# Block masks turned two heads at a time and copied under the queries, filter work moved to other engines and earlier heads

## The chip, the cores and the metric

The kernel runs on one core of a Trainium2 chip. The metric is the time of one execution on the device in microseconds (us), lower is better, as a median of several runs. A core has five engines that follow their own instruction lists in order: TensorE (PE, matmuls), VectorE (DVE), ScalarE (ACT), GpSimd (POOL) and SyncE (SP), which here only issues DMAs. Engines wait for one another by semaphores. DMAs issued by SP share one hardware queue; those issued by POOL go through another.

## The reference

Two stages. The first is causal block-sparse attention: 4 batches of 8 heads, 768 positions, head size 64, so 32 heads in all. Keys are averaged in 12 blocks of 64. Each query scores the 12 block means, keeps the three best blocks that are not ahead of it and its own block, and attends to the keys in those blocks up to its own position:

```python
gate_scores = np.where(causal, einsum('bhsd,bhnd->bhsn', q, k_rep), -1e9)
top_idx = np.argsort(gate_scores, axis=-1)[..., -3:]   # and the own block
scores = np.where(mask & causal_by_position, scale * q @ k.T, -1e9)
attn_out = softmax(scores) @ v
```

The heads are put side by side (4 x 768 x 512) and go to the second stage, which convolves with a filter over the positions:

```python
x1, x2, x3 = split(x @ w_proj, 3)                   # 512 columns each
x2_conv = irfft(rfft(x2, axis=1) * rfft(filter_fft, axis=0))
out = (x1 * x2_conv * x3) @ w_out
```

## The kernel before, in words

**Attention, one head.** A head takes three slots, and a loop over all slots writes out the order of the work on every engine by hand. The 768 positions lie in six chunks of 128. In slot 0 of head n the loop issues loads for later heads, and for head n+3 `split_query` (DVE: a 16-bit query and its rest), `cast_key` and `low_query` (POOL: the 16-bit key, and the rest scaled). These land in `qk16`, of which there are three: per chunk 128 columns of query (64 high, 64 low) and 128 of key (64 of key, 12 that hold a one-hot of the key's block times 16384, zeros). In slot 1 `turn_query(n+3)` (L315) turns `qk16` by a DMA so that features lie on partitions: `qkT`, five buffers. In the same slot `gate(n+2)` (L331 to L343) multiplies the turned queries with the block sums of the keys (high and low halves give the precision that the choice of blocks needs), takes the best three on DVE and writes 0 or -1 per block into `qm16`, columns 64 to 75, beside a copy of the query that POOL makes (`mask_query`, L319). In slot 2 `turn_mask(n+2)` (L348) turns `qm16`, six blocks of 128x128, by another DMA.

`scores` (L375) multiplies 76 rows of the turned keys with 76 rows of the turned masked queries, so that a block that was not chosen gets -16384 before the exp. The scores are computed keys by queries, in three groups, one per slot, of 1024, 896 and 768 columns. ScalarE takes the exp (L378), POOL clears what lies ahead on the diagonal blocks (`diagonals`, L386), PE multiplies with the values in the next slot (`product`, L397), with a column of ones for the sums, ScalarE takes the inverse of the sums (L404, L405) and DVE scales (L415).

**Block sums.** `key_sums_mm`, `key_sums_copy`, `key_sums_turn`, `key_sums_split` prepare the sums for a group of heads: head 0, heads 1 to 3, 4 and 5, 6 and 7, then by fours.

**Second stage.** Its units are listed by slot in `first_plan` for batch 0, from slot 29 (slot 2 of head 9) to slot 49, and in `plan` for the others, 24 slots each. X2 projects x2, F1 and F2 are the forward and inverse transforms as matmuls with cosine and sine matrices, X13 projects x1 and x3, O is the output product. What they need is made by a table `setup` of (head, slot): `filter_rows` (L570 to L572) folds the filter's rows, `filter_spectrum` (L578 to L587) transforms them and writes the spectrum `Asb`, `Bsb`, `weights` (L596) loads and casts columns of the weights by POOL's DMAs, `inverse_part` (L234, L236) turns the cosine and sine matrices by DMA. The loop emits in a slot: scores, what earlier slots left for `later` (POOL's `PQ` and `yT` products among it), diagonals, the attention work above, `setup`, the units, and the product of the slot before.

**Queues.** SP issues in program order; an issue waits until its data is ready, and what follows on SP waits with it. PE, POOL, DVE and ScalarE are in order too.

Of the kernel before, what the change touches and what calls it, by code (L numbers as in the profile page):

```python
# [9 lines left out]
FP32 = mybir.dt.float32  # L10
# [7 lines left out]
def kernel(  # L18
# [76 lines left out]
    key_groups = [[0], [1, 2, 3], [4, 5], [6, 7]] + [list(range(m, m + KG))  # L95
# [20 lines left out]
    load_query(0)  # L116
    load_key(0)
    load_key(1)
    load_query(1)
    load_value(0)  # L120
    load_key(2)
    load_key(3)
# [28 lines left out]
    qk16s, qm16s, v16s = [], [], []  # L151
    for i in range(NB):
        qk16 = const.tile([P, SC, 2, P], fp, name=f"qk16_{i}")
        qk16s.append(qk16)
        qm16s.append(const.tile([P, SC, P], fp, name=f"qm16_{i}"))
        v16s.append(const.tile([P, SC, P], fp, name=f"v16_{i}"))

    def key_mask(i):
        nc.gpsimd.tensor_scalar(qk16s[i][:, :, 1, D:D + NBLK], in0=eblk, scalar1=MASK, scalar2=0.0,
                                op0=ALU.mult, op1=ALU.add)  # L160
# [7 lines left out]
    cbias = const.tile([P, SC, NBLK], FP32)  # L168

    ownm = const.tile([P, SC, NBLK], FP32)  # L170
# [3 lines left out]
    def small_constants():  # L174
        nc.gpsimd.memset(cbias, 0.0)
        nc.gpsimd.affine_select(
            out=cbias[0:64], in_=cbias[0:64], compare_op=ALU.is_ge,
            fill=-CBIG, base=0, pattern=[[2, SC], [-1, NBLK]], channel_multiplier=0)
        nc.gpsimd.affine_select(
            out=cbias[64:128], in_=cbias[64:128], compare_op=ALU.is_ge,  # L180
            fill=-CBIG, base=1, pattern=[[2, SC], [-1, NBLK]], channel_multiplier=0)
        nc.gpsimd.tensor_scalar(ownm, in0=eblk, scalar1=1.0, scalar2=-1.0,
                                op0=ALU.mult, op1=ALU.add)
# [31 lines left out]
    def sines(i):  # L215
# [3 lines left out]
        if i == 0:  # L219
# [76 lines left out]
    def cast_key(n):  # L296
        g, i = group_of[n]
        nc.gpsimd.tensor_copy(qk16s[n % NB][:, :, 1, 0:D], keys[g][:, i])
# [3 lines left out]
    def split_query(n):  # L302
        qk16 = qk16s[n % NB]
        q_nat = queries.pop(n)
        nc.vector.tensor_copy(qk16[:, :, 0, 0:D], q_nat)  # L305
        rems[n] = remp.tile([P, SC, D], FP32, name="rem", tag="rem")
        nc.vector.tensor_sub(rems[n], q_nat, qk16[:, :, 0, 0:D])  # L307

    def low_query(n):
        nc.gpsimd.tensor_scalar(qk16s[n % NB][:, :, 0, D:P], in0=rems.pop(n), scalar1=LO, scalar2=0.0,  # L310
                                op0=ALU.mult, op1=ALU.add)

    def turn_query(n):
        turned[n] = augp.tile([P, SC, 2, P], fp, name="qkT", tag="qkT")
        nc.sync.dma_start_transpose(turned[n].rearrange("p c t s -> p (c t) s"),  # L315
                                    qk16s[n % NB].rearrange("p c t s -> p (c t s)"))

    def mask_query(n):
        nc.gpsimd.tensor_copy(qm16s[n % NB][:, :, 0:D], qk16s[n % NB][:, :, 0, 0:D])  # L319
# [7 lines left out]
    def gate(n):  # L327

        gps = one_tile("gps", (P, GC * 2 * NBLK)).rearrange("p (c t n) -> p c t n", c=GC, t=2)
        for c in range(GC):  # L330
            nc.tensor.matmul(gps[:, c, :, :], lhsT=turned[n][:, c + 1, 0, :],  # L331
                             rhs=sums[group_of[n][0]][:, group_of[n][1], :, :],
                             start=True, stop=True)
        ga = small.tile([P, GC, NBLK], FP32, name="ga", tag="ga")
        nc.vector.tensor_add(ga, gps[:, :, 0, :], cbias[:, 1:SC, :])
        g = small.tile([P, GC, NBLK], FP32, name="g", tag="g")
        nc.vector.tensor_add(g, gps[:, :, 1, :], ga)
        m8 = small.tile([P, GC, 8], FP32, name="m8", tag="m8")
        for c in range(GC):
            nc.vector.max(m8[:, c, :], g[:, c, :])  # L340
        get = small.tile([P, GC, NBLK], FP32, name="get", tag="get")
        nc.vector.tensor_tensor(get, g, m8[:, :, 2:3].to_broadcast([P, GC, NBLK]), op=ALU.is_ge)
        nc.vector.scalar_tensor_tensor(out=qm16s[n % NB][:, 1:SC, D:D + NBLK], in0=get, scalar=-1.0,  # L343
                                       in1=ownm[:, 1:SC, :], op0=ALU.add, op1=ALU.max)

    def turn_mask(n):
        masks[n] = augp.tile([P, SC, P], fp, name="qmT", tag="qmT", bufs=4)
        nc.sync.dma_start_transpose(masks[n], qm16s[n % NB].rearrange("p c s -> p (c s)"))  # L348
# [21 lines left out]
    def scores(n, gi):  # L370
        pieces, lo, hi, _ = groups[gi]
        qT = masks[n].rearrange("p c s -> p (c s)")
        sps = big_tile("sps")
        for kc, qs, qe, col in pieces:
            nc.tensor.matmul(sps[:, col:col + qe - qs], lhsT=turned[n][0:76, kc, 1, :],  # L375
# [191 lines left out]
    def filter_rows(i):  # L567
# [3 lines left out]
        nc.vector.tensor_add(fil[:, 0, i, :], fa, rev)  # L571
        nc.vector.tensor_sub(fil[:, 1, i, :], fa, rev)  # L572

    def filter_spectrum(j):
# [9 lines left out]
        def put(dst, first, s0, second, s1, op):  # L584
            t = p2b.tile([P, Dm], FP32, name="turn", tag="t1")
            nc.vector.tensor_scalar(t, in0=second, scalar1=s1, scalar2=None, op0=ALU.mult)
# [16 lines left out]

    at(2, 1, turn_weights)
    at(4, 2, make_flip)
    for i in range(HC):
        at(i, 2, cosines, i)
        at(5 + i, 2, load_rows, i)
        at(7 + i, 0, filter_rows, i)
        at(10 + i, 2, inverse_part, i, False)  # L610
        at(10 + i, 2, inverse_part, i, True)
    for i, (n, slot) in enumerate([(9, 1), (10, 2), (11, 1)]):
        at(n, slot, filter_spectrum, i)
    for i in range(DC):
        dsl = slice(P * i, P * (i + 1))
        at(6 + (i + 1) // 2, 1, weights, wp, moe_w_proj, slice(Dm, 2 * Dm), slice(i, i + 1))
        n = [9, 10, 11, 12][i]
        at(n, 0, weights, wp, moe_w_proj, slice(P * i, P * (i + 1)), slice(0, DC))
        at(n, 1, weights, wp, moe_w_proj, slice(2 * Dm + P * i, 2 * Dm + P * (i + 1)), slice(0, DC))
        at(12 + i, 2, weights, wo, moe_w_out, slice(0, Dm), slice(i, i + 1))  # L620


    turn_angles()
    nc.vector.memset(lsc, 1.0)
    nc.vector.memset(lsc[64:128, :], 1.0 / LO)
    for i in range(NB):
        nc.vector.memset(qk16s[i][:, :, 1, D + NBLK:P], 0.0)
# [12 lines left out]
    load_query(2)  # L640
    key_sums_mm(0, range(SC))
    key_sums_copy(0)
    key_sums_turn(0)
    sines(1)
    small_constants()
    key_sums_split(0)
    phase_round(2)
    phase_turns(2)
    key_mask(1)
    split_query(1)  # L650
    cast_key(1)
    low_query(1)
    turn_query(1)
    load_key(4)
    load_key(5)
    key_sums_mm(1, range(SC))
    sines(2)
    nc.scalar.activation(tw, twf, AF.Sin, bias=0.0, scale=math.pi / S)

    nc.scalar.preload_act_table_set("natural_log_exp_and_others")  # L660
    for i in range(NB):
        nc.gpsimd.memset(qm16s[i][:, :, D:P], 0.0)
    mask_query(0)
    gate(0)
    turn_mask(0)
    nc.gpsimd.memset(v16s[0][:, :, D:P], 1.0)
    cast_value(0)
    key_mask(2)
    load_query(3)
    load_value(1)  # L670
    key_sums_copy(1)
    key_sums_turn(1)
# [4 lines left out]
    key_sums_split(1)  # L677
    gate(1)
    mask_query(1)
    turn_mask(1)  # L680
    for i in range(1, NB):
        nc.gpsimd.memset(v16s[i][:, :, D:P], 1.0)
    mask_query(2)
# [4 lines left out]
    for slot in range(max(units) + 1):  # L688
# [10 lines left out]
        if n < NH:  # L699
            diagonals(n, s)  # L700
            if s == 0:
# [3 lines left out]
                if n + 4 < NH:  # L705
                    load_query(n + 4)
# [4 lines left out]
                if n + 3 < NH:  # L711
                    split_query(n + 3)
                    cast_key(n + 3)
                    low_query(n + 3)
                if n + 2 in group_at and n:
                    key_sums_split(group_at[n + 2])
            elif s == 1:
                if n + 3 < NH:
                    turn_query(n + 3)
                if n + 2 < NH:  # L720
                    gate(n + 2)
            else:
                if n + 2 < NH:
                    turn_mask(n + 2)
                if n + 3 < NH:
                    mask_query(n + 3)
# [55 lines left out]
```

## Time and profile before

| | us |
|---|---|
| median of three runs | 330.61 |
| lowest, highest | 329.84, 330.74 |
| the profiled execution, in all | 328.21 |
| its span | 326.5 |
| mean granted clock of PE | 0.932 of full |

| engine | busy us | share of the span |
|---|---|---|
| PE | 256.4 | 79% |
| DVE | 227.2 | 70% |
| ACT | 196.3 | 60% |
| POOL | 191.5 | 59% |

The profile is one execution. Its page gives busy time by engine, the span in 40 equal slices, the chain of work that ended last, and the costliest groups of instructions. L with a number is a line of the kernel. Other views list the waits, the instructions in order of time, or the busy time in a stretch. "DMA share" is the mean busy share of the 16 DMA engines; as it sums the time of packets that overlap, it can pass 1. Times in the text such as "scores of head 10 at 93.6" are starts from the span's beginning, read from the timeline.

### The profile page before, as it was taken

The page shows a single profiled execution, that of the slowest core. Times are in us where ns is not written, and L with a number is a line of the kernel's source. Part 1 is how long each engine was busy: PE and PEld are TensorE (multiplying, and loading weights), DVE is VectorE, ACT ScalarE, POOL GpSimd, SP SyncE. Part 2 cuts the span into 40 slices and gives each one's busy share as a digit, 9 for nine tenths or more (in the row PEclk, how much of TensorE's full clock was granted, in tenths as well). Part 3 has the DMA queues.
Part 4 walks back from the last instruction along what each step waited for, and adds up shares of the span by engine and source line. Part 5 has one row for each costly group of instructions (what it writes and reads, how often), then busy time and mean ns, then how long its engine had stood idle before and what let it go on. Part 6 is the DMA issues. An engine that isn't in the chain of part 4 may idle for free.

```text
span 326.5 us, 5163 instructions
## 1 busy us (share of the span) xinstructions
PE 256.4 (79%) x1531; PEld 132.9 (41%) x1531; DVE 227.2 (70%) x637; ACT 196.3 (60%) x314; POOL 191.5 (59%) x360
## 2 busy tenths in 40 slices
PE   3567687665989585995499787997997889899785
PEld 2233333232344242552144444553444446445442
DVE  6557867535799994689247898788678976537650
ACT  2247787663445453586367956688867669943234
POOL 6646747644244778576534587678645876703770
PEclk9959989775899998999589999999999999999999
DMA  9999999999999959797677977687996471021005
GB/s 168 182 206 181 217 218 199 201 219 218 167 147 158 145 103 177 154 132 151 135 163 168 214 151 160 113 140 155 220 200 156 99 125 24 2 103 58 34 1 193
DMA packets 163260, 48.65 MB, mean 149 GB/s; under 512 B 158368, under 2 KB 159392, under 8 KB 163232
## 3 DMA queue, kind: packets, MB, share of 16 engines
q1 hardware_dynamic: 157856, 46.22, 72.6%
q0 software_dynamic: 5376, 2.10, 6.0%
q8 instruction: 12, 0.20, 0.2%
q14 instruction: 16, 0.13, 0.1%
HBM read 24.64 MB, written 6.29 MB: 95 GB/s over the span
## 4 chain that ended last, share of the span: by engine, by line
PE 44%; DVE 18%; DMA 14%; ACT 8%; issue 7%; POOL 6%; SPq 1%; DVEq 0%; ACTq 0%; POOLq 0%
DMA qkT<-qk 10%; PE oT L397 7%; PE krp L266 6%; PE sps L375 5%; PE op L515 5%; PE x13b L482 4%; PE x2a L443 3%; PE x2b L443 3%; PE x13a L482 2%; DVE xT L415 2%; ACT den L404 2%; ACT ex L378 2%; ACT den L405 2%; DVE gx L487 2%; DVE t L464 2%
## 5 line engine op out<-in xcount | busy, mean ns | idle before, releaser
L378 ACT ACTIVATE ex<-sps 128x1024 f16<-128x1024 f32 (+2 forms) x96 | 87.4, 917 | 30.5 <-PE sps L375 28.5
L386 POOL TENSOR_SCALAR_AFFINE_SELECT ex<-ex 128x128 f16<-128x128 f16 (+1 forms) x128 | 46.7, 377 | 82.7 <-ACT ex L378 81.8
L397 PE MATMUL oT<-ex,v 128*128 128x384 f16 (+2 forms) x288 | 57.7, 308 | 3.7 <-POOL ex L386 1.9
L375 PE MATMUL sps<-qmT,qkT 76*128 76x384 f16 (+2 forms) x288 | 57.0, 311 | 0.9 <-DMA qmT<-qm 0.9
L415 DVE TENSOR_TENSOR xT<-oT,den 64x384 f16<-64x384 f32 x64 | 35.2, 550 | 27.8 <-ACT den L405 26.3
L404 ACT ACTIVATE den<-oT 64x384 f32<-64x384 f32 x64 | 31.1, 485 | 37.8 <-PE oT L397 35.8
L397 PEld LDWEIGHTS <-v 128*128 128x128 f16 x288 | 27.4, 102 | 39.0 <-issue 20.8
L482 PEld LDWEIGHTS <-wp 128*128 128x128 f16 x256 | 24.3, 97 | 28.9 <-issue 14.0
L405 ACT ACTIVATE den<-den 64x384 f32<-64x384 f32 x64 | 33.3, 520 | 2.0
L266 PE MATMUL krp<-k_nat,eblk 128*12 128x256 f32 (+3 forms) x120 | 29.2, 382 | 5.3 <-issue 2.0
L375 PEld LDWEIGHTS <-qkT 76*128 76x128 f16 x288 | 27.2, 104 | 13.0 <-issue 3.4
L515 PE MATMUL op<-wo,yT 128*128 128x512 f16 x96 | 25.6, 392 | 8.1 <-DMA wo<-in_moe_w_out_dram 6.1
L482 PE MATMUL x13b<-xT,wp 128*128 128x384 f16 x116 | 23.6, 326 | 6.1 <-ACT x1sb L486 4.0
L471 POOL TENSOR_TENSOR PQ<-t,t 128x512 f16<-128x512 f32 x12 | 15.2, 1271 | 21.0 <-DVE t L464 20.6
L482 PE MATMUL x13a<-xT,wp 128*128 128x384 f16 x116 | 23.6, 326 | 4.1 <-DVE t L467 3.9
L305 DVE CAST qk<-q_nat 128x384 f16<-128x384 f32 x32 | 18.8, 587 | 10.9 <-issue 4.5
L518 ACT COPY osb<-op 128x512 f32<-128x512 f32 x24 | 14.0, 585 | 18.7 <-PE op L515 17.6
L307 DVE TENSOR_TENSOR rem<-q_nat,qk 128x384 f32<-128x384 f32 x32 | 22.8, 714 | 2.4
L310 POOL TENSOR_SCALAR qk<-rem 128x384 f16<-128x384 f32 x32 | 16.3, 510 | 11.1 <-DVE rem L307 8.9
L331 PE MATMUL gps<-kr,qkT 128*128 128x24 f16 x160 | 9.1, 176 | 16.8 <-DMA qkT<-qk 15.8
L507 POOL TENSOR_TENSOR yT<-gx,yy 128x384 f16<-128x384 f32 x16 | 16.0, 999 | 10.0 <-DVE yy L503 9.7
L486 ACT CAST x1sb<-x13a 128x384 f16<-128x384 f32 x29 | 13.8, 476 | 12.4 <-PE x13a L482 12.4
(122 smaller groups left out, 432.3 us busy)
## 6 DMA issues: line engine op xcount, KB each, us to landing
q_nat<-in_q_dram SPq DMA_DIRECT2D x32, 192.0 KB, 3.5
k_nat<-in_k_dram SPq DMA_DIRECT2D x32, 192.0 KB, 3.2
v_nat<-in_v_dram SPq DMA_DIRECT2D x32, 192.0 KB, 3.7
out_dram<-osb SPq DMA_DIRECT2D x24, 256.0 KB, 2.1
wp<-in_moe_w_proj_dram POOLq DMA_DIRECT2D x12, 128.0 KB, 5.1
fa<-in_moe_filter_fft_dram SPq DMA_DIRECT2D x3, 256.0 KB, 3.1
fb<-in_moe_filter_fft_dram SPq DMA_DIRECT2D x3, 256.0 KB, 4.1
qkT<-qk SPq DMA_TRANSPOSE x32, 4.4
```

What stands on the lines that cost most here:

```text
L266: nc.tensor.matmul(sums[g][0:NBLK, 0:w * D], lhsT=eblk[:, c, :], rhs=keys[g][:, 0:w, c, :], start=(c == 0), stop=(c == SC - 1))
L307: nc.vector.tensor_sub(rems[n], q_nat, qk16[:, :, 0, 0:D])
L375: nc.tensor.matmul(sps[:, col:col + qe - qs], lhsT=turned[n][0:76, kc, 1, :], rhs=qT[0:76, qs:qe], start=True, stop=True, skip_group_check ...
L378: nc.scalar.activation(ex[:, lo:hi], sps[:, lo:hi], AF.Exp, bias=0.0, scale=scale)
L386: nc.gpsimd.affine_select(out=sub, in_=sub, compare_op=ALU.is_ge, fill=0.0, base=0, pattern=[[0, cnt], [1, P]], channel_multiplier=-1)
L397: nc.tensor.matmul(oT[:, qs - HALF * half:qe - HALF * half], lhsT=vals[n][:, kc, :], rhs=exps[n, src][:, col:col + qe - qs], start=first, ...
L404: nc.scalar.activation(den[64:128, :], oT[64:128, :], AF.Ln, bias=0.0, scale=1.0)
L405: nc.scalar.activation(den[64:128, :], den[64:128, :], AF.Exp, bias=0.0, scale=-1.0)
L415: nc.vector.tensor_tensor(out=dst, in0=oT[0:64, :], in1=den[64:128, :], op=ALU.mult)
L443: nc.tensor.matmul(pp, lhsT=xT[:, dc, base + P * i:base + P * (i + 1)], rhs=wp[:, dc, Dm:2 * Dm], start=(dc == 0), stop=(dc == DC - 1))
L482: nc.tensor.matmul(dst, lhsT=wp[:, dc2, base:base + P], rhs=xT[:, dc2, hs:hs + HALF], start=(dc2 == 0), stop=(dc2 == DC - 1))
L515: nc.tensor.matmul(op, lhsT=yT[:, cc, P * scn:P * (scn + 1)], rhs=wo[:, cc, :], start=(cc == 0), stop=(cc == DC - 1))
```

## The change

**Masks.** `gate` takes a list of one or two heads and writes their masks side by side into `gm16` (24 columns, two buffers); one DMA (`turn_mask`) turns both. The turned query's low half is needed by the gate alone, so its rows 64 to 75 are then overwritten with the mask rows by a small DMA within the core's memory (`place_mask`, 12 partitions x 768), and `scores` reads the turned query itself. `qm16` and POOL's `mask_query` are gone. Heads 0 and 1 have their masks turned on PE and copied by ScalarE (`turn_first_mask`). From then on, for even n, heads n+2 and n+3 share `gate` (slot 1 of head n) and `turn_mask` (slot 2); their two `place_mask` stand in slot 1 of head n+1. For heads 2 and 3 gate and turn stand in slot 2 of head 0.

**Order.** Queries and keys are prepared four heads ahead and not three; the queries' layout is by kind and then chunk. Loads at the start are query and key of heads 0, 1, 2 first, and the key groups become [0], [1], [2, 3], and so on.

**Filter.** ScalarE copies the flipped rows out of PSUM, POOL adds and subtracts; in the spectrum ScalarE does the product that DVE did. These run in heads 4 to 8 in place of 7 to 11, the cosine and sine turns in heads 8 to 10 (before 10 to 12), the weights' columns in heads 8 to 11 (before 9 to 12), the output weights in heads 11 to 14 (before 12 to 15).

```diff
-    key_groups = [[0], [1, 2, 3], [4, 5], [6, 7]] + [list(range(m, m + KG))
+    key_groups = [[0], [1], [2, 3], [4, 5], [6, 7]] + [list(range(m, m + KG))
...
-    load_query(0)
-    load_key(0)
-    load_key(1)
-    load_query(1)
-    load_value(0)
-    load_key(2)
-    load_key(3)
+    for n in range(3):
+        load_query(n)
+        load_key(n)
...
     def turn_query(n):
-        turned[n] = augp.tile([P, SC, 2, P], fp, name="qkT", tag="qkT")
-        nc.sync.dma_start_transpose(turned[n].rearrange("p c t s -> p (c t) s"),
-                                    qk16s[n % NB].rearrange("p c t s -> p (c t s)"))
-
-    def mask_query(n):
-        nc.gpsimd.tensor_copy(qm16s[n % NB][:, :, 0:D], qk16s[n % NB][:, :, 0, 0:D])
+        turned[n] = augp.tile([P, 2, SC, P], fp, name="qkT", tag="qkT")
+        nc.sync.dma_start_transpose(turned[n].rearrange("p t c s -> p (t c) s"),
+                                    qk16s[n % NB].rearrange("p t c s -> p (t c s)"))
...
-    def turn_mask(n):
-        masks[n] = augp.tile([P, SC, P], fp, name="qmT", tag="qmT", bufs=4)
-        nc.sync.dma_start_transpose(masks[n], qm16s[n % NB].rearrange("p c s -> p (c s)"))
+    def turn_mask(ns):
+        gmT = augp.tile([P, SC, P], fp, name="gmT", tag="gmT", bufs=2)
+        nc.sync.dma_start_transpose(gmT, gm16s[(ns[0] + len(ns)) // 2 % 2].rearrange("p c s -> p (c s)"))
+        for h, n in enumerate(ns):
+            masks[n] = gmT[h * NBLK:(h + 1) * NBLK]
+
+    def turn_first_mask(n):
+
+        gmp = ps_one.tile([P, S], fp, name="gmp", tag="one", padded_shape=[P, 2 * 512])
+        for c in range(SC):
+            nc.tensor.transpose(gmp[0:NBLK, P * c:P * (c + 1)],
+                                gm16s[(n + 1) // 2 % 2][:, c, 0:NBLK], id_f16)
+        nc.scalar.copy(turned[n][D:D + NBLK, 0],
+                       gmp[0:NBLK, :].rearrange("n (c s) -> n c s", c=SC))
+
+    def place_mask(n):
+
+
+        nc.sync.dma_start(turned[n][D:D + NBLK, 0], masks.pop(n))
...
-        qT = masks[n].rearrange("p c s -> p (c s)")
+        qT = turned[n][:, 0].rearrange("p c s -> p (c s)")
...
-        nc.vector.tensor_add(fil[:, 0, i, :], fa, rev)
-        nc.vector.tensor_sub(fil[:, 1, i, :], fa, rev)
+        nc.scalar.copy(fb, rev)
+        nc.gpsimd.tensor_add(fil[:, 0, i, :], fa, fb)
+        nc.gpsimd.tensor_sub(fil[:, 1, i, :], fa, fb)
...
-            nc.vector.tensor_scalar(t, in0=second, scalar1=s1, scalar2=None, op0=ALU.mult)
+            nc.scalar.mul(t, second, s1)
...
+    at(0, 2, gate, [2, 3])
+    at(0, 2, turn_mask, [2, 3])
...
-        at(5 + i, 2, load_rows, i)
-        at(7 + i, 0, filter_rows, i)
-        at(10 + i, 2, inverse_part, i, False)
-        at(10 + i, 2, inverse_part, i, True)
-    for i, (n, slot) in enumerate([(9, 1), (10, 2), (11, 1)]):
-        at(n, slot, filter_spectrum, i)
+        at(2 + i, 2, load_rows, i)
+        at(4 + i, 1, filter_rows, i)
+        at(6 + i, 2, filter_spectrum, i)
+        at(8 + i, 2, inverse_part, i, False)
+        at(8 + i, 2, inverse_part, i, True)
...
-        n = [9, 10, 11, 12][i]
+        n = 8 + i
...
-        at(12 + i, 2, weights, wo, moe_w_out, slice(0, Dm), slice(i, i + 1))
+        at(11 + i, 2, weights, wo, moe_w_out, slice(0, Dm), slice(i, i + 1))
...
-                if n + 4 < NH:
-                    load_query(n + 4)
+                if n + 5 < NH:
+                    load_query(n + 5)
...
-                if n + 3 < NH:
-                    split_query(n + 3)
-                    cast_key(n + 3)
-                    low_query(n + 3)
+                if n + 4 < NH:
+                    split_query(n + 4)
+                    cast_key(n + 4)
+                    low_query(n + 4)
...
-                if n + 3 < NH:
-                    turn_query(n + 3)
-                if n + 2 < NH:
-                    gate(n + 2)
+                if n + 4 < NH:
+                    turn_query(n + 4)
+                if n % 2 == 0 and 0 < n < NH - 2:
+                    gate([n + 2, n + 3])
+                elif n % 2 == 1 and n + 1 < NH:
+                    place_mask(n + 1)
+                    place_mask(n + 2)
             else:
-                if n + 2 < NH:
-                    turn_mask(n + 2)
-                if n + 3 < NH:
-                    mask_query(n + 3)
+                if n % 2 == 0 and 0 < n < NH - 2:
+                    turn_mask([n + 2, n + 3])
```

## The prediction

> **What bounds the kernel now.** I read the page's slices, then the chain of waits in order of time, then the span cut head by head (busy time by stretch), last the timelines of SP, POOL and PE around one head. The columns of the first view are 40 slices of 8.2 us.
>
> ```profile
> PEclk9959989775899998999589999999999999999999
> DMA  9999999999999959797677977687996471021005
> ```
>
> For the first 14 slices (to about 115 us) the DMA engines are full, while the units of the second part start only in slot 2 of head 9. The chain says what the queue holds up:
>
> ```profile
> 22.44 5.06 DMA qkT<-qk
> 28.06 5.51 DMA qkT<-qk
> 34.59 4.41 DMA qkT<-qk
> ...
> 52.75 5.95 DMA qkT<-qk
> 59.88 6.26 DMA qkT<-qk
> ...
> 68.59 6.57 DMA qkT<-qk
> ...
> 124.49 4.20 DMA IC<-FC
> ...
> 156.66 3.00 DMA wo<-in_moe_w_out_dram
> ```
>
> To 75 us the end is set by the turns of queries and keys (T(n), L315): `gate(n+2)`, in slot 1 of head n, waits for T(n+2). After that single DMAs stand in the chain: the IC turn, and the last `wo` weight.
>
> Below, one stretch per head, from its first scores matmul to the next head's: heads 11, 13, 15, 16, then 19, 21, 23, 24, which have the same units one batch later (19 as 11, and so on). Columns: length, then busy us of PE, PEld, DVE, ACT, POOL, the clock, DMA share, GB/s.
>
> ```profile
> 103.00:115.20 12.20, 8.54 (x52) 4.27 (x50) 11.49 (x27) 5.24 (x8) 7.64 (x12) 1.00 0.97 156
> ...
> 124.60:137.90 13.30, 10.73 (x60) 5.18 (x58) 6.88 (x21) 6.20 (x10) 8.39 (x15) 0.87 0.97 158
> ...
> 144.90:152.40 7.50, 5.03 (x40) 3.01 (x38) 7.20 (x16) 4.31 (x8) 5.48 (x10) 1.00 0.76 157
> 152.40:167.40 15.00, 8.91 (x41) 4.12 (x39) 6.01 (x18) 7.59 (x12) 7.35 (x14) 0.66 0.77 157
> ```
> ```profile
> 183.30:191.80 8.50, 6.54 (x46) 3.69 (x44) 7.48 (x21) 6.22 (x10) 5.99 (x10) 1.00 0.76 165
> ...
> 201.90:211.10 9.20, 9.20 (x60) 4.65 (x58) 7.20 (x21) 6.19 (x10) 7.55 (x14) 1.00 0.67 130
> 211.10:218.10 7.00, 6.45 (x50) 3.84 (x48) 5.97 (x19) 5.85 (x10) 4.44 (x10) 1.00 0.85 121
> 218.10:223.80 5.70, 5.01 (x39) 3.00 (x37) 5.41 (x15) 4.28 (x9) 5.26 (x10) 1.00 0.81 165
> 223.80:231.60 7.80, 6.42 (x42) 3.16 (x39) 5.88 (x17) 6.89 (x12) 5.60 (x10) 1.00 0.92 198
> ```
>
> Heads 10 to 16 take 73.9 us. Their twins: head 10's three units cost as head 18 (6.8) and a little more, 7.5; head 12 as head 20 (10.1) less one output unit (0.9), 9.2; then 8.5, 9.2, 7.0, 5.7, 7.8: together 55. So 19 us of heads 10 to 16 are filter work, the wait for IC (head 13) and the 6.1 us that PE waits for `wo` (head 16).
>
> **The change part by part.** My sum is against the profiled execution: 326.5 us span, 328.21 in all, which is 2.4 below the median of the runs.
>
> *Heads 0 and 1.* The first mask loses its DMA turn (issued 14.62, landed 17.69) and takes six PE transposes (nearest row L282, 0.21 each) and a ScalarE copy of 768 columns (nearest row an exp of 768, 0.81). But both first masks now stand ahead of the first scores on PE: the gate of head 1, its 1.9 us on DVE, then six more transposes. POOL's identity and larger constants (about 1 us) lie beside DVE's work. I put the first scores at 18 us, as now (17.7); bounds 16.5 and 20.
>
> *Heads 2 to 9.* Loads come as 256-byte packets (192 KB: 768), and T(n) is 12 blocks of 128 rows, 1,536 packets; the old mask turn is 768. That makes 4,608 per head, 147,456 of the page's 157,856 on queue 1. Up to T(3), 1,248 packets per engine, landed 27.5; up to T(8), 2,736, landed 58.7: 21 ns each, 6.0 us per head. Now a pair needs one mask turn instead of two: 528 per engine for two heads, 11.1 us instead of 12.1. That is the gain. The loss is what must be through the queue before a head starts. Today the scores of head n need T(n+1). Now `place_mask` for heads n+1 and n+2 is issued in slot 1 of odd head n, on SP behind T(n+4); the scores of n+1 wait for it, and PE with them. Head 2 thus needs everything up to T(5): 1,536 per engine, 1.5 + 32.1 = 33.6, and about 1.3 for the copy: 35, today 30.1.
>
> From there it is a loop and no longer a stream: T(n+4) waits for POOL's `low_query(n+4)`, which stands behind the diagonal masks of head n's slot 0, so behind its scores and exp. In head 23:
>
> ```profile
> 222.05 0.50 POOL L298 CAST qk<-k_nat 128x384 f16<-128x384 f32 x1
> 222.64 0.51 POOL L310 TENSOR_SCALAR qk<-rem 128x384 f16<-128x384 f32 x1
> ```
> ```profile
> 223.18 1.44 SPq L315 DMA_TRANSPOSE qkT<-qk  x1
> ```
>
> Scores 218.1, `low_query` done 223.15, T issued 223.18, landed 226.85; the scores of head 24 began at 223.81, and with the copy behind T would have to wait past 227. So an odd head lasts at least (scores to `low_query`) + (T's issue to the copy's landing). The first is 4.0 to 5.7 in the odd heads read from the timelines (4.0, 4.5, 5.3, 4.8 in heads 1 to 7; 5.7 in 15; 5.0 in 23). The second is in no row. T itself lands 3.6 after issue at best, 4.4 in the median, 9.0 at worst; the nearest row for the copy is an output store, 2.0 at best after its own issue, and the copy's issue is 1.5 behind T's. So at least 3.6; I take 4.2 where the queue is free, being T's row plus one more item, and 5 in the early heads; upper bound 9.5.
>
> The Trainium skill, page "DMA: Bandwidth & Descriptors", section "Anatomy of one DMA — SWDGE (gpsimd) path", gives every DMA a fixed cost of about 2 us whatever its bytes, fitted on the software path, and so speaks against small copies; the 18 KB copy would by that be an estimated 2.04 us, 3.5 behind T's issue, each of some eleven odd heads 0.7 shorter than I reckon, and the sum below −12.7 in place of −5.0. No run here shows a copy of this size.
>
> Early odd heads then last 9.5 (4.5 + 5), even ones about 5 (head 2: 30.1 to 35.1 today): 14.5 per pair instead of the stream's 12.1. Heads 4 and 6 add a `rev` product (L570, 1.8 us of PE), 6 and 8 a filter spectrum (six matmuls, 1.6), and heads 8 and 9 the weights (1.4 us of queue each): pairs of 14.5, 16, 16, 16.5 from head 2. Scores of head 10 at 98, today 93.6: +4.4. With the queue empty at each copy the stream could be at 94; with 1 us more in each pair, 102.
>
> *Filter, by engine.* POOL's add and subtract (nearest row L471, 1.27 each, three pairs: 7.6) sit in slot 1 of heads 4 to 6 and may push `low_query` of the next head by 1 or so; ScalarE's copies (0.58 each) and seven products lie under the same waits. SP's third pair of row loads waits for POOL's first pair. All costed at nothing because the copy's wait covers them; without that cover, some 5 us.
>
> *Heads 10 to 16.* The filter is gone from here (7 `turn` and 7 `put` on DVE, 10 us, on the path in heads 9, 11); IC and IS turns come two heads sooner, `wo` one head sooner, ahead of the `yT` products that hold POOL at 153 to 156. So 73.9 becomes 55, but with the odd head's least time: head 11, 4.0 + 4.2, +1 for the weights in the queue; head 13, 5.2 + 4.2 against 9.2; head 15, 5.75 less `mask_query` (0.6, off POOL) + 4.2 = 9.3 against 5.7. Together 60: −13.9.
>
> *Heads 17 to 31.* `mask_query` leaves POOL (19.1 us in all) and the paired gate saves DVE 0.2 per head, neither on the path, which is PE's. The copy's wait: head 23, 5.0 − 0.6 + 4.2 = 8.6 against 5.7, +2.9; head 25, T landed 6.4 after issue among output stores, +1.6; heads 17, 19, 21, 27 between 7.9 and 8.6, against 8.5 to 9.2, nothing; 29 has no T ahead. +4.5; bounds 0 and 10. The tail from 285 is untouched.
>
> Sum: +4.4 − 13.9 + 4.5 = −5.0: 323.2, and by the median of the runs 325.6.
>
> **Rivals.**
> *The copy binds harder (slower).* If T's issue to the copy's landing takes 1.5 more than I reckon, 5.7 and early 6.5 (T lands 4.4 to 6.6 in the chain above), four early pairs lose 6 us and heads 11 to 27 about 10: 325.6 + 16 = 341.6. It decides from about 0.5 us later than I reckon, since some eleven heads carry it. For it: the early turns. Against: after 160 us T lands 3.7 in most heads.
> *The copy is hidden (much faster).* If POOL reaches `low_query` 2 us sooner, head 10 starts at 94 and the later waits vanish: −19, so 312. Against: POOL waits for ScalarE's exp (81.8 us of its idle time), not for itself.
> *The filter disturbs the early heads.* POOL holds `low_query` behind the filter's waits for PE, ScalarE and the row loads: 5 to 6 us more by head 10, about 331, no change.
>
> **How the numbers follow.** Forecast 0.5, harder copy 0.22, hidden copy 0.15, disturbed 0.13. About 0.3% (1 us) is what a measurement can tell from no change. Faster: 0.47 + 0.15 + 0.04; same 0.03 + 0.05 + 0.02; slower the rest. Range: below, half of the hidden case is left out, 315; above, most of the harder one is kept, 335. The likeliest case alone runs from 320 to 330.
>
> **What would show it.** Right: scores of head 2 near 35, of head 10 near 98, of head 17 near 158; PE idle before the scores of even heads until the copy lands; no wait for `wo` or IC. Wrong: the even heads' scores do not wait, or T's issue to the copy's landing is over 5 in heads 17 to 27; heads 10 to 16 over 64 us.

## The result, and the profile after

The changed kernel takes 347.8 us (median; 345.0 to 349.3), the kernel before, run beside it, 330.2. The ratio is 1.054 with a 95% interval of 1.045 to 1.064: 5% slower, where 325.6 was forecast and 335 was the upper end. The profiled execution has a span of 345.7 us and a mean granted clock of 0.904 (before 326.5 and 0.932). Times here and below are medians of all executions, while the ratios leave out the few executions in a slower state, at most two of a run.

First the page of the changed kernel: clock and DMA share in 40 slices, now of 8.6 us, and the shares of the chain that ended last.

```profile
PEclk9996876787769699899969999999699999999999
DMA  8796979998569889768778686667866511021004
...
PE 42%; POOL 14%; ACT 13%; DVE 11%; DMA 10%; issue 7%; SPq 4%; DVEq 0%; ACTq 0%; POOLq 0%
```

The row of DMA shares no longer begins with fourteen nines: the stream that bounded the first 115 us is gone. The clock row has the new trouble, a 6, 7 or 8 in most slices from 26 to 112 us. The next view is the list of waits: waiting engine and line, what it waited for, then the total in us, how often, and the longest.

```profile
PE sps L393 <- DMA qkT<-gmT: 33.8, 10, 6.0
...
DVE qk L302 <- DMA q_nat<-in_q_dram: 10.2, 2, 7.7
```

PE waits 33.8 us for the small copy of the mask rows under the turned queries (`qkT<-gmT`). The chain of waits has that copy ahead of head after head; its columns are start, length and what was waited for:

```profile
39.04 2.18 DMA qkT<-gmT
...
55.46 2.10 DMA qkT<-gmT
...
71.86 2.26 DMA qkT<-gmT
...
91.28 4.37 DMA qkT<-gmT
...
112.48 3.29 DMA qkT<-gmT
...
133.76 5.77 DMA qkT<-gmT
...
172.68 2.39 DMA qkT<-gmT
...
239.78 2.36 DMA qkT<-gmT
...
272.75 2.39 DMA qkT<-gmT
```

Before each of them lies what SP did. In SP's timeline of head 11 ("SPq" is the queue's own issue) the copies leave when the issue of the next queries' turn T(15) is done, although their mask had been turned a head earlier:

```profile
131.03 2.63 SPq L312 DMA_TRANSPOSE qkT<-qk  x1
133.76 2.06 SPq L366 DMA_DIRECT2D qkT<-gmT  x2
```

The scores of head 12 start at 139.58, 8.6 us after T's issue. The forecast beside the measured, in starts of first scores and in lengths (us):

| | before | forecast | after | missed by |
|---|---|---|---|---|
| scores of head 2 start | 30.1 | 35 | 41.3 | 6.3 |
| heads 2 and 3 | 13.0 | 14.5 | 16.4 | 1.9 |
| heads 4 and 5 | 11.3 | 16 | 16.6 | 0.6 |
| heads 6 and 7 | 13.5 | 16 | 21.5 | 5.5 |
| heads 8 and 9 | 25.6 | 16.5 | 20.1 | 3.6 |
| heads 10 to 16 | 73.8 | 60 | 67.7 | 7.7 |
| head 17 to the end | 159.0 | 163.5 | 162.2 | −1.3 |
| span | 326.5 | 321.5 | 345.7 | 24.2 |

So three quarters of the miss lies in front of head 10. A stage read from one execution is good to 1 us at best: a later run, the same program up to head 8, has that head's scores at 94.9, the changed kernel at 95.7. In the early heads of the kernel before it is worse: the filter's half alone (below), the same program up to slot 2 of head 2, reaches head 2 at 32.7 and not 30.1.

### The profile page after: what moved, and what is told of

Same layout as the page of the kernel before. It is cut to its first block, busy times and chain, and to the rows that moved or that the text cites. A ratio compares the mean times of both kernels' runs of the same rounds, so it can differ in the third digit from the quotient of the medians.

```text
span 345.7 us, 5124 instructions
## 1 busy us (share of the span) xinstructions
PE 268.8 (78%) x1555; PEld 138.3 (40%) x1555; DVE 206.4 (60%) x568; ACT 204.4 (59%) x326; POOL 186.1 (54%) x336
## 4 chain that ended last, share of the span: by engine, by line
PE 42%; POOL 14%; ACT 13%; DVE 11%; DMA 10%; issue 7%; SPq 4%; DVEq 0%; ACTq 0%; POOLq 0%
DMA qkT<-gmT 8%; PE sps L393 7%; PE oT L415 6%; PE op L533 5%; ACT ex L396 4%; PE krp L263 4%; SPq L312 3%; ACT den L422 3%; PE x2a L461 3%; PE x2b L461 2%; POOL ex L404 2%; PE x13b L500 2%; PE x13a L500 2%; ACT den L423 2%; POOL PQ L489 1%
## 5 line engine op out<-in xcount | busy, mean ns | idle before, releaser
L396 ACT ACTIVATE ex<-sps 128x1024 f16<-128x1024 f32 (+2 forms) x96 | 88.0, 917 | 59.4 <-PE sps L393 57.4
L393 PE MATMUL sps<-qkT 76*128 76x384 f16 (+2 forms) x288 | 62.2, 332 | 33.8 <-DMA qkT<-gmT 33.8
L415 PE MATMUL oT<-ex,v 128*128 128x384 f16 (+2 forms) x288 | 59.7, 314 | 11.6 <-POOL ex L404 6.5
L263 PE MATMUL krp<-k_nat,eblk 128*12 128x256 f32 (+2 forms) x132 | 28.3, 356 | 1.9 <-POOL dft_ka L205 1.6
L533 PE MATMUL op<-wo,yT 128*128 128x512 f16 x96 | 27.2, 416 | 2.0 <-POOL yT L525 1.8
L500 PE MATMUL x13a<-xT,wp 128*128 128x384 f16 x116 | 24.3, 332 | 0.0
L302 DVE CAST qk<-q_nat 128x384 f16<-128x384 f32 x32 | 17.9, 559 | 10.4 <-DMA q_nat<-in_q_dram 10.2
L505 DVE TENSOR_TENSOR gx<-x1sb,x13b 128x384 f32<-128x384 f16 x29 | 16.0, 551 | 12.5 <-PE x13b L500 8.3
L304 DVE TENSOR_TENSOR rem<-q_nat,qk 128x384 f32<-128x384 f32 x32 | 21.2, 664 | 2.5
L317 POOL CAST v<-v_nat 128x384 f16<-128x384 f32 x32 | 19.0, 593 | 0.0
```

Of the source, the lines that this page charges most:

```text
L263: nc.tensor.matmul(sums[g][0:NBLK, 0:w * D], lhsT=eblk[:, c, :], rhs=keys[g][:, 0:w, c, :], start=(c == 0), stop=(c == SC - 1))
L304: nc.vector.tensor_sub(rems[n], q_nat, qk16[:, 0, :, 0:D])
L317: nc.gpsimd.tensor_copy(vals[n][:, :, 0:D], values.pop(n))
L396: nc.scalar.activation(ex[:, lo:hi], sps[:, lo:hi], AF.Exp, bias=0.0, scale=scale)
L415: nc.tensor.matmul(oT[:, qs - HALF * half:qe - HALF * half], lhsT=vals[n][:, kc, :], rhs=exps[n, src][:, col:col + qe - qs], start=first, ...
L500: nc.tensor.matmul(dst, lhsT=wp[:, dc2, base:base + P], rhs=xT[:, dc2, hs:hs + HALF], start=(dc2 == 0), stop=(dc2 == DC - 1))
```

## The experiments

The expectations call the theory that the copies' place behind T sets the time C, and the theory that the moved filter work does it F, with numbers for their variants. Two more came out of the trace: the first heads wait for query 4's load, and PE runs at half clock after each wait. Ratios below are to the kernel before, run beside each, with 95% intervals. Its median lay between 328.9 and 331.4 us in these rounds, so one or two microseconds between runs of different rounds mean little.

### The copies ahead of T

In slot 1 of odd heads the two copies are issued before the turn of queries n+4:

```diff
             elif s == 1:
+                if n % 2 == 1 and n + 1 < NH:
+                    place_mask(n + 1)
+                    place_mask(n + 2)
                 if n + 4 < NH:
                     turn_query(n + 4)
                 if n % 2 == 0 and 0 < n < NH - 2:
                     gate([n + 2, n + 3])
-                elif n % 2 == 1 and n + 1 < NH:
-                    place_mask(n + 1)
-                    place_mask(n + 2)
```

> The changed kernel, with one order turned round: in slot 1 of odd heads the two mask copies are issued on SP ahead of the query turn T(n+4) instead of behind it. Theory C (the copy behind T is the cost): PE's waits for the copy before even heads, 33.8 us in ten waits, shrink to under 8 us in all; 347.8 falls by 20 to 33, to 315 to 328. Rival F (the filter on POOL and ScalarE in heads 4 to 8 holds the early heads): the waits turn into waits for other work, the time stays over 338. Rival S (the start alone is late): head 2 still starts near 39 to 41 and less than 10 us are gained.

Measured: 323.3 us, ratio 0.974 [0.968, 0.980]. Two lines changed places, and 24.5 us are gone: the change is now 2.6% faster than the kernel before. SP's timeline of this run, in slot 1 of head 11:

```profile
120.31 1.59 SPq L366 DMA_DIRECT2D qkT<-gmT  x2
122.00 2.24 SPq L312 DMA_TRANSPOSE qkT<-qk  x1
```

In the kernel as changed the copies sat out T's own issue (2.6 us in this head) and, in heads such as 7, 15 and 23, T's wait for POOL's `low_query` before it. Here they leave 1.7 us before T does, in head 13 3.1. Head 15 shortens from 9.4 to 6.6 us, head 23 from 8.8 to 5.7 (before: 7.5 and 5.7). The waits of this run:

```profile
PE sps L393 <- DMA qkT<-gmT: 14.7, 5, 4.0
```

They were to fall below 8 and fell to 14.7. What is left are the waits of heads 2, 4, 6, 10 and 12, and in the chain of this run their copies take longer than any quiet one above:

```profile
36.35 3.57 DMA qkT<-gmT
...
51.05 3.70 DMA qkT<-gmT
...
65.70 4.41 DMA qkT<-gmT
...
100.91 5.12 DMA qkT<-gmT
...
120.31 5.11 DMA qkT<-gmT
```

Loads, turns and weights are in the queues at that time; which of these holds the copies was not tried. By stage the swap is worth 1.3 by the start of head 2, then 8.4 in heads 2 to 9, 10.3 in heads 10 to 16, and 6.3 in the rest. That last stage is now 155.9 against 159.0 before, about 1 us less in each of heads 19, 24 and 27. The filter's half alone leaves it at 159.0, so the 3.1 us are what the masks' half is worth there once nothing waits; `mask_query`, the halved gates and the longer lead were not tried apart.

### Each half alone

The masks' half alone has the change, but the filter's engines and slots of the kernel before:

```diff
-        nc.scalar.copy(fb, rev)
-        nc.gpsimd.tensor_add(fil[:, 0, i, :], fa, fb)
-        nc.gpsimd.tensor_sub(fil[:, 1, i, :], fa, fb)
+        nc.vector.tensor_add(fil[:, 0, i, :], fa, rev)
+        nc.vector.tensor_sub(fil[:, 1, i, :], fa, rev)
...
-            nc.scalar.mul(t, second, s1)
+            nc.vector.tensor_scalar(t, in0=second, scalar1=s1, scalar2=None, op0=ALU.mult)
...
-        at(2 + i, 2, load_rows, i)
-        at(4 + i, 1, filter_rows, i)
-        at(6 + i, 2, filter_spectrum, i)
-        at(8 + i, 2, inverse_part, i, False)
-        at(8 + i, 2, inverse_part, i, True)
+        at(5 + i, 2, load_rows, i)
+        at(7 + i, 0, filter_rows, i)
+        at(10 + i, 2, inverse_part, i, False)
+        at(10 + i, 2, inverse_part, i, True)
+    for i, (n, slot) in enumerate([(9, 1), (10, 2), (11, 1)]):
+        at(n, slot, filter_spectrum, i)
```

with the slots of the weights and of `make_flip` back as well. The filter's half alone is the same edit the other way round, on the kernel before.

> The masks' half of the change alone: masks of two heads in one turn and the copies stay, while the filter's work, its engines, the weights and the cosine and sine turns stand where they were before the change. Theory C: the copy's waits stay, the relief of heads 10 to 16 is gone, so 350 to 360, slower than the whole change. Rival F: without the filter in heads 4 to 8 scores of head 10 come 9 us or more sooner than 115.8 and the time is under 346.

> The other half alone: the kernel before, with its masks and query turns, and only the filter folded by ScalarE and POOL in heads 4 to 8, the cosine and sine turns two heads sooner and the weights one head sooner. Theory C: this half is a gain by itself, as the sum had it: the waits for wo and IC go, head 10 starts by 96, heads 10 to 16 last 56 to 60 instead of 73.9; 314 to 322. Rival F: POOL's part holds the query turns of heads 5 to 9, head 10 starts after 100, and the time is 325 or more.

Masks alone: 342.9 us, 1.034 [1.027, 1.040]. Filter alone: 321.6 us, 0.970 [0.964, 0.977]. The first is 7 us better than C gave it and inside the time that F gave it, though head 10 comes only 6.9 us sooner (109.0), not 9: the moved filter costs something where the masks' half has made a loop. The two halves multiplied make 1.003, the whole 1.054: the 5%, some 17 us, belong to neither half but to their meeting. By the intervals that is roughly 12 to 21 us. In the four profiled spans it is 8.9: 6.6 in heads 2 to 9 and 6.0 in heads 10 to 16, less 3.2 ahead of head 2, where single executions differ as said above, and 0.6 at the end. Drawing the filter and the weights forward costs 0.8 us in heads 2 to 9 of the kernel before (64.3 for 63.5), which go by the DMA stream, and 7.4 with the new masks (74.5 for 67.1). Read from the start of head 10 it is 3.4 (97.0 for 93.6) and 6.9 (115.8 for 109.0); the direction is the same, the size is good to a few microseconds.

The filter alone gave 9.0 us in heads 10 to 16 (64.8 for 73.8) where 56 to 60 was expected of that stage, and head 10 by 96. The wait for `wo` is gone, and a smaller one for POOL's `yT` has come, in PE's timeline of that run, the product in head 16:

```profile
154.38 0.81 PE L515 MATMUL op<-wo,yT 128*128 128x512 f16 x3
155.76 0.39 PE L515 MATMUL op<-wo,yT 128*128 128x512 f16 x1 [0.57 <-POOL yT L507]
```

### The start

Scores of head 0 begin at 18.8, but head 0 then lasts 12.5 us, twice as long as before (6.2). DVE's timeline of the changed kernel (in brackets: idle time before, and what ended it):

```profile
18.38 0.56 DVE L304 TENSOR_TENSOR rem<-q_nat,qk 128x384 f32<-128x384 f32 x1
...
26.64 0.36 DVE L302 CAST qk<-q_nat 128x384 f16<-128x384 f32 x1 [7.70 <-DMA q_nat<-in_q_dram]
```

`split_query(4)` stands in slot 0 of head 0 and waits 7.7 us for a load that SP issued at 22.6, behind T(3) and two keys. Everything after it on DVE waits too: the block sums of heads 2 and 3, then their gate. The load is moved up:

```diff
     turn_query(2)
+    load_query(4)
     load_value(1)
...
     load_key(5)
-    load_query(4)
```

> The changed kernel, with the load of query 4 issued after the query turn of head 2, ahead of that of head 3 and of keys 4 and 5. Rival S: DVE's 7.7 us wait for query 4 in head 0 goes, head 2 starts at 35 to 37 instead of 41.3, and the time falls by 3 to 6, to 342 to 345. Theory C: head 2 starts sooner, but the loop of turn and copy keeps its pace and hardly any of it is lost later: also 342 to 346. If head 2 does not move, DVE's wait was covered by the DMA stream and the time stays at 347 to 349.

> Both orders at once on the changed kernel: the copies ahead of the turn, and the load of query 4 ahead of the turn of head 3. If the two losses are apart, 323.3 falls by another 4 to 6, to 317 to 320, and head 2 starts near 36. If head 0's wait is covered by something else once the copies are early, no change from 323.

Alone: 341.9 us, 1.033 [1.025, 1.041], 5.9 less than the change as it was. The line of DVE's timeline:

```profile
21.61 0.36 DVE L302 CAST qk<-q_nat 128x384 f16<-128x384 f32 x1 [2.63 <-DMA q_nat<-in_q_dram]
```

Head 2 starts at 37.7 and not 41.3, where 35 to 37 was expected. Together with the copies ahead of T: 320.7 us, 0.972 [0.968, 0.975], 2.6 less than that edit alone, where 4 to 6 were expected. In its trace head 2 starts 3.9 sooner and head 10 only 2.7: a part of an earlier start is taken back on the way.

### PE's clock after a wait

After the long waits PE runs at half clock. PE's timeline of the changed kernel at the start of head 10:

```profile
115.81 1.01 PE L393 MATMUL sps<-qkT 76*128 76x128 f16 x4 [5.37 <-DMA qkT<-gmT]
...
117.28 1.89 PE L461 MATMUL x2a<-wp,xT 128*128 128x512 f16 x4
118.95 1.91 PE L461 MATMUL x2b<-wp,xT 128*128 128x512 f16 x4
...
122.35 1.02 PE L461 MATMUL x2a<-wp,xT 128*128 128x512 f16 x4
123.21 1.03 PE L461 MATMUL x2b<-wp,xT 128*128 128x512 f16 x4
```

Four matmuls of one form take 1.89 us after the wait and 1.02 five us later; the four of the scores take 1.01. The same head in the last but one run below (the version without dummies), where it starts after no wait to speak of:

```profile
98.07 0.60 PE L393 MATMUL sps<-qkT 76*128 76x128 f16 x4 [0.17 <-DMA qkT<-gmT]
...
98.94 1.04 PE L461 MATMUL x2a<-wp,xT 128*128 128x512 f16 x4
99.82 1.03 PE L461 MATMUL x2b<-wp,xT 128*128 128x512 f16 x4
...
101.65 1.02 PE L461 MATMUL x2a<-wp,xT 128*128 128x512 f16 x4
```

The second `x2a` stands 3.6 us behind the scores here and 6.5 in the changed kernel, and head 10 lasts 8.6 us here and 11.6 there. The same matmuls stand between in both, each of them longer there: the 3.0 are the clock. By the clock's records half clock lasts 68.5 us of this span, 46.6 before. Is it a cost or only an accompaniment? Ten matmuls, whose results nobody reads, fill PE's wait ahead of eight even heads:

```diff
         sps = big_tile("sps")
+        if gi == 0 and n in (2, 4, 6, 8, 10, 12, 16, 24):
+            for _ in range(10):
+                nc.tensor.matmul(sps[:, 0:F], lhsT=id_f16, rhs=FS[:, 0, :], start=True, stop=True,
+                                 skip_group_check=True)
```

As a control the same ten stand ahead of eight odd heads, which have no such wait:

```diff
-        if gi == 0 and n in (2, 4, 6, 8, 10, 12, 16, 24):
+        if gi == 0 and n in (3, 5, 7, 9, 11, 13, 17, 25):
```

> The changed kernel with ten extra matmuls of 128 x 384 on constants (4.1 us at half clock, 1.6 at full) ahead of the scores of heads 2, 4, 6, 8, 10, 12, 16 and 24, where PE waits for the copy; they write the tile that the scores then overwrite, and do nothing else. Theory K (a part of the loss is PE at half clock after each of these waits: 68.5 us at half clock against 46.6 before): the half-clock time falls under 55 us and the time by 3 to 8, to 340 to 345, though PE has more to do. If the clock costs nothing because the path runs over DMA, POOL and ScalarE, the time stays at 346 to 352.

> Control for the extra matmuls: the changed kernel with the same ten matmuls, eight times, but ahead of the scores of heads 3, 5, 7, 9, 11, 13, 17 and 25, where PE does not wait for a copy. Theory K: nothing covers them there; they hold back the odd head's scores, and with them exp, low_query and the turn on the loop, by 1.6 to 3.2 us each: 348 to 358. If extra matmuls help wherever they stand, because they lift the clock in general: 335 to 343 here too.

Ahead of the even heads: 335.4 us, 1.015 [1.010, 1.020]: 12.4 us less for 80 matmuls more, where 3 to 8 were expected, and 40.5 us at half clock. The dummies run into the wait. In head 2 the scores after them run at full clock, in head 10 they do not:

```profile
36.16 1.79 PE L394 MATMUL sps<-FS,id_f 128*128 128x384 f16 x10
41.01 0.60 PE L397 MATMUL sps<-qkT 76*128 76x128 f16 x4 [3.06 <-DMA qkT<-gmT]
...
106.86 1.79 PE L394 MATMUL sps<-FS,id_f 128*128 128x384 f16 x10
111.61 1.01 PE L397 MATMUL sps<-qkT 76*128 76x128 f16 x4 [2.97 <-DMA qkT<-gmT]
```

Head 2 starts no sooner than without them (41.0 for 41.3): the copy comes when it comes. It is the heads after the waits that get shorter: head 2 from 5.15 to 4.68, head 6 from 8.97 to 7.68, head 8 from 6.78 to 5.02, head 12 from 9.88 to 8.34, head 16 from 8.40 to 6.11, head 24 from 8.99 to 6.11. Two of the eight gain nothing, head 4 (6.8 both times) and head 10 (11.6): there the scores began 3.17 and 2.97 us after the last dummy and took 1.01 again. Head 2's began 3.06 after theirs and took 0.60, so the length of that gap alone does not decide; by the clock's records half clock came there a little later, from 42.9 to 49.7. (The waits for the copy fall from 33.8 to 16.9 us in the list, but the dummies stand in them for 14.4 of that; that fall by itself says nothing.)

Ahead of the odd heads: 348.8 us, 1.060 [1.053, 1.066], as slow as without them, though the mean clock rose from 0.904 to 0.921 and half clock fell to 57.0 us. In its trace heads 2 to 9 gain 2.7 and heads 10 to 16 lose 4.1. So it isn't the load on PE but its place, in the wait, that brings the gain.

The kernel before has a 6, 7 or 8 in the clock row as well, over its early heads. There 24 matmuls of 128x120 go ahead of the gate of heads 3 to 10:

```diff
+        if 3 <= n <= 10:
+            for _ in range(24):
+                nc.tensor.matmul(gps, lhsT=FS[:, 0, 0:P], rhs=FS[:, 0, 0:GC * 2 * NBLK],
+                                 start=True, stop=True)
```

> The kernel before, with 24 extra matmuls of 128 x 120 on constants ahead of the gate of heads 3 to 10, where PE waits for the query turns (46.6 us at half clock). If the early heads there go by the DMA stream (21 ns a packet), a faster PE gains nothing: 328 to 332. If the half clock was part of the path before as well: 320 to 326.

Measured: 330.9 us, 1.0035 [1.0002, 1.0068]. The clock rose from 0.932 to 0.958, its half-clock time fell from 46.6 to 29.1 us, and nothing was won. So in these two kernels a low clock costs where PE's work starts the next step of the loop, and nothing that shows where a DMA stream sets the pace. One reservation: in heads 3, 4 and 7 the 24 matmuls (1.4 to 1.8 us) leave no wait after them and may hold the gate back a little; that this hides a small gain is not excluded.

### The filter's engines, and the weights in the queue

The change with only the engines of the filter back on DVE, slots as changed:

```diff
-        nc.scalar.copy(fb, rev)
-        nc.gpsimd.tensor_add(fil[:, 0, i, :], fa, fb)
-        nc.gpsimd.tensor_sub(fil[:, 1, i, :], fa, fb)
+        nc.vector.tensor_add(fil[:, 0, i, :], fa, rev)
+        nc.vector.tensor_sub(fil[:, 1, i, :], fa, rev)
...
-            nc.scalar.mul(t, second, s1)
+            nc.vector.tensor_scalar(t, in0=second, scalar1=s1, scalar2=None, op0=ALU.mult)
```

> The changed kernel with only the filter's engines undone: fold and spectrum products on DVE as before the change, in the new slots (heads 4 to 8). Theory F1 (ScalarE, which waits for DVE's turn buffer in head 6, slot 2, and POOL with 2.5 us of fold, hold exp and low_query on the loop): heads 4 to 9 get 4 to 8 us shorter together and the time falls to 340 to 344, to the level of the masks alone (342.9). Rival F2 (it is the slots, PE's 1.9 us of rev and the spectrum's matmuls, not the engines): within 1.5 us of 347.8.

Measured: 343.1 us, 1.034 [1.028, 1.040]: 4.7 less. In the profile heads 4 to 9 are 2.9 shorter together, where 4 to 8 were expected. How the filter gets into the loop is seen in the chain of the changed kernel, from the flipped rows in head 6 to the copy that head 8 waits for:

```profile
77.26 1.91 PE rev L588 x2
79.20 0.59 ACT fb L589
79.86 1.29 POOL fil L590
81.16 1.23 POOL fil L591
...
82.85 0.70 ACT turn L605
83.57 0.76 DVE Asb L606
84.40 0.70 ACT turn L605
85.12 0.76 DVE Bsb L606
85.91 0.69 ACT turn L605
86.60 0.91 ACT ex L396
...
89.20 0.52 POOL qk L307
90.08 1.10 SPq L312
91.28 4.37 DMA qkT<-gmT
```

ScalarE's products wait for DVE between two of them (0.87 and 0.82 us in its timeline), since DVE works on what the product before made. The exp of head 7 stands behind them on ScalarE, POOL's `low_query` behind that exp, T behind `low_query` and the copy behind T.

In heads 8 to 11 the weights' columns go through POOL's DMA queue. In the chain the copy takes 2.1 to 2.4 us in heads 1, 3, 5, 15, 23 and 27, but 4.4, 3.3 and 5.8 in heads 7, 9 and 11. So the loads of heads 9 and 11 are moved into the even heads before them:

```diff
-        n = 8 + i
+        n = 8 + i // 2 * 2
```

> The changed kernel, with the weights' column loads of heads 9 and 11 moved one head ahead, to heads 8 and 10, where no copy is issued. In the changed kernel T's issue to the scores took 7.1 us in head 9 and 8.6 in head 11, against 4.0 in heads 19 and 27. If the weights' load of the DMA engines makes the difference: 5 to 6 us in both, each head 2 to 3 us shorter, and the time at 341 to 345. If it is the query, key and value loads and the sine and cosine turns ahead of them: 7 to 8.6 as now, and 347 to 349.

Measured: 342.6 us, 1.038 [1.030, 1.046]: 5.3 less. SP's timeline in head 11, and PE's at the start of head 12:

```profile
129.70 1.91 SPq L312 DMA_TRANSPOSE qkT<-qk  x1
131.71 1.91 SPq L366 DMA_DIRECT2D qkT<-gmT  x2
```
```profile
135.38 1.03 PE L393 MATMUL sps<-qkT 76*128 76x128 f16 x4 [2.51 <-DMA qkT<-gmT]
```

From T's issue to the scores are now 5.7 us, not 8.6; in head 9 4.9, not 7.1. Head 11 lasts 9.3, not 12.2. Head 9 lasts 12.7, not 13.3, where 2 to 3 less were expected: its T leaves 7.9 us after the head's first scores and not 6.2, because the issue of a value load ahead of it on SP took 2.5 us instead of 0.7. The four other runs with the copies behind T and the weights where the change has them (query 4 sooner, both runs with dummies, the filter on DVE) show from T's issue to the scores 6.3 to 6.7 us in head 9 and 6.2 to 8.4 in head 11, so what the weights cost there is less than these two traces alone say.

### All together

Copies ahead of T, query 4 sooner and the filter's folding on DVE, and then also the dummies ahead of heads 2, 4, 6 and 12:

```diff
+        if gi == 0 and n in (2, 4, 6, 12):
+            for _ in range(10):
+                nc.tensor.matmul(sps[:, 0:F], lhsT=id_f16, rhs=FS[:, 0, :], start=True, stop=True,
+                                 skip_group_check=True)
```

> All three on the changed kernel: copies first, query 4 sooner, filter on DVE in the new slots. If the three losses are apart: 312 to 316, the fastest so far. If with the copies early the filter's engines no longer lie on the path: as with the two orders alone, 317 to 320.

> Copies first, query 4 sooner, filter on DVE, and ten extra matmuls ahead of the scores of heads 2, 4, 6 and 12, where PE still waits 0.9 to 4.7 us. If the clock still costs there: 314 to 317, half-clock time under 25 us (29.6 without). If these stages now go by the DMA queue: 317 to 319, no gain.

Without dummies: 317.9 us, 0.964 [0.959, 0.968]. That is inside the second expectation, though 2.8 less than the two orders alone gave. With them: 315.1 us, 0.956 [0.951, 0.962], 32.7 us under the change as it was, and faster than both kernels. That the dummies gave the last 2.8 is not shown: the intervals overlap, half clock fell only from 29.6 to 26.8 us, and of the 1.9 us between the two spans 1.5 lie in head 24, ahead of which none stand. The clock row of the last run:

```profile
PEclk9996699899869999999799999999999999999999
```

## Why the prediction was wrong

It named the right mechanism, and its nearest rival, "The copy binds harder", had the right sign and gave 341.6. The forecast put its own terms too low, one by one, held one at nothing that lies on the path, and left out the clock.

**"Head 2 thus needs everything up to T(5) ... 35, today 30.1."** Measured 41.3, 6.3 more. The step counted packets in the queue and left out in which order DVE takes its work. Four heads of lead put `split_query(4)` into head 0, ahead of the gate of heads 2 and 3, and its load had been issued last. 3.6 of the 6.3 come back with the load moved alone, 5.2 with the copies moved as well.

**"An odd head lasts at least (scores to `low_query`) + (T's issue to the copy's landing)."** As a lower bound this law held, and undoing it by the swap gave 24.5 us. Its first term, reckoned at 4.5 early, measures 4.5 in heads 1, 3 and 5, but 6.6 in head 7 and 5.0 in head 9. Between its terms lies one that it lacks: in heads 1, 3 and 9 T left 0.9, 1.7 and 1.2 us after the end of `low_query`, because SP was still issuing turns and loads. Its second term was "4.2 where the queue is free" and "5 in the early heads". From T's issue to the scores the late heads that wait for the copy (15, 19, 23, 27) measure 3.9 to 4.1, as reckoned. The early ones measure 4.7, 5.1, 5.3, 6.0, 7.1 and 8.6 (heads 1, 3, 5, 7, 9, 11). In heads 1, 3 and 5 the issue of T alone is 2.4 to 2.9 of that, against 1.4 in the late heads. The last two have the weights in the queue, and moving these took off 2.3 and 2.9: the forecast put "+1 for the weights" on head 11 and its 9.2 became 12.2, which went to 9.3 when the loads were moved. The 6.0 of head 7 has weights beside it too; that these are its cause is argued from heads 9 and 11, not shown.

The estimate beside this step from the Trainium skill was 2.04 us for the copy, from a fixed cost of some 2 us that the skill gives for DMAs on the software path ("DMA: Bandwidth & Descriptors", section "Anatomy of one DMA — SWDGE (gpsimd) path"). This copy goes by SP's queue; its rows in heads 1, 3, 5, 15, 23 and 27, 2.1 to 2.4 from its own issue, are near that, those of heads 7, 9 and 11 are not.

**"All costed at nothing because the copy's wait covers them."** This was the step that failed in its reasoning. The filter's work isn't beside the copy's wait: rev, ScalarE's copy, POOL's folding and the products stand ahead of the exp and of `low_query`, whose end starts T, whose issue starts the copy. It lies in series with the loop. Heads 6 and 7 last 21.5 us and not 16. The slots and engines together cost 7.4 us in heads 2 to 9 with the new masks, 2.9 of it the choice of engines; under the old stream 0.8 (6.9 and 3.4 by the start of head 10). The forecast's own "without that cover, some 5 us" was near.

**A term that the sum lacked: the clock.** PE's wait was counted once, as the time until the copy lands. It is paid a second time in the head after it, at half clock. Filling the waits gave 12.4 us over the whole kernel; in the profile 3.9 of it in heads 2 to 9, 4.6 in heads 10 to 16, 2.9 after. It overlaps with the other terms, since a wait that is gone costs no clock either.

**"73.9 → 55 by twins, 60 with the odd head's least time"** (in short). The reading by twins was right: with the copies ahead of T heads 10 to 16 take 57.4, and the waits for `wo` and IC are gone. Head by head the forecast's terms add to 59.4, and 8.3 are missing: 4.1 in head 10, of which 3.0 are the half clock after its wait; 3.0 in head 11, of which 2.9 went with the weights' loads moved; heads 12 to 16 were off by 1.2 together.

**Heads 17 to 31, +4.5.** Measured +3.2 (162.2 for 159.0). Right in size and in place: head 23 was forecast at 8.6 and lasts 8.8. What it left out is the 3.1 that the masks' half gives there when the copy does not wait. Whether "neither on the path" was wrong, or the longer lead gives them, stays open.

**The chances.** The rival's condition, "from about 0.5 us later than I reckon", was passed in heads 7, 9 and 11 (6.0, 7.1 and 8.6, forecast at 5, 5 and 5.2). Against it the forecast set the late heads, "after 160 us T lands 3.7 in most heads". That was true, and of the heads where the time was lost it said nothing. Of its own signs of being wrong one came: heads 10 to 16 took 67.7, over 64.

## What to carry to other kernels

On an in-order queue the price of a small transfer is what stands ahead of its issue: here a copy behind a turn that had to wait for POOL cost 24.5 us, and two lines changing places paid for it. When a change turns a stage from a stream into a loop of waits, the work that the stream covered is no longer free; cost it again as a link of the loop, engine by engine, in each engine's own order. And a wait of several microseconds on PE is to be counted with the half-clock time after it.

## What the hardware showed that was not expected

How much the half clock costs was not expected: 12.4 of 347.8 us, shown by 80 added matmuls. After a wait of 5.4 us the same four matmuls took 1.89 us instead of 1.02. In the changed kernel the first four matmuls of the scores took 0.8 to 1.0 us after each of the eight waits of 2.7 us and more, and 0.61 after the two of 0.5 and 0.6. In the control, with the dummies elsewhere, the clock's mean rose by 0.017 and the time did not fall.

The Trainium skill describes this on the page "TensorE: Matmul & The Clock Gate", section "HAM oscillation — how this bites in real kernels": waits for DMAs of some 3 to 5 us throttle PE again, so that each next burst starts cold. The rows here agree with that.

And a higher mean clock alone is no gain: on the kernel before it went from 0.932 to 0.958 with a ratio of 1.0035.
